# A 32-byte tile ahead of all others on the right-hand side of SBUF

## The chip, the cores and the metric

The kernel runs on one core of a Trainium2 chip. The metric is the time of one execution on the device, in microseconds. Before the change the median of three runs is 992.73 us (992.7 to 994.15).

## The reference

Three layers follow each other, all in float32.

```
phi(x) = exp(h - max h) / sqrt(128),  h = x @ omega.T - |x|^2/2      # 4 x 8 heads, 576 tokens, 64 wide
num, den = phi(q) @ (phi(k).T @ v),  phi(q) @ sum phi(k)
x = num / (den + 1e-6)                                               # 2304 tokens x 512
h = x @ w_in;  x = (max(h,0) + alpha * min(h,0)) @ w_out             # hidden width 2048
out = ((x @ w_a) * (x @ w_b)) @ w_out                                # hidden width 1536
```

## The kernel before

Every large product keeps float32 accuracy by splitting each operand into a high and a low part (`hi`, `lo`, type float32r) and adding three products, high x high, high x low and low x high. A hidden tile of 128 columns costs 12 matmuls in the first layer (line 440: four 128-row pieces of x, three products each) and 12 in the second (line 498). Such twelve are called a block below. The weights of both MLPs come in as raw bits and are taken apart by a decoder (the class at line 165) on GpSimd, VectorE and ScalarE into slots, each `[128, 2, 512]` float32r: high part first, low part 2048 bytes behind it.

The work goes through four stages.

- 0 to about 256 us: linear attention (lines 651 to 758) with the first MLP's earliest chunks between its steps, 256 tokens at a time (object `A`, pools on the left).
- Up to about 551 us: the rest of the first MLP (object `X`, line 994), in chunks of 512 tokens and one of 256. Two chunks of 512 use hidden tiles 0 to 7; then four of 512 and one of 256 use hidden tiles 8 to 15.
- Up to 988 us: the second MLP, in 3 x 3 rounds. In each, two calls of `dual` make 7 products of 12 matmuls with 384 columns (line 1067); `back` then makes six groups of 12 matmuls with 512 columns (line 1138), which read a weight slot as the moving operand and the 384-column tiles `gh` and `gl` as the stationary one.

The order of every engine is the program's own order (`manual_schedule`); queues and waits follow from it.

Where the tiles lie is decided by pools. SBUF is filled from two sides. On the left stand the constants, the weight slots 0 to 16 (pool `w1`), the decoder's tiles, x, and the pools of object `A`; in the second MLP also the x pieces of the products A11, S1 and S2 (pool `xa`). On the right, from the top downwards, stand all attention tiles; after them the weight slots 17 to 24 (`w2`) and all pools of object `X`; after these the slots 25 and 26 (`w3`) and the other pools of the second MLP. Each stage's pools are stacked from the same top.

Which slot a weight tile q has is said by `place`: q below 20 has slot q, 20 to 24 have 20 to 24, and 25 to 31 have slots 0 to 6. Hidden tile f of the first MLP uses q = 2f in line 440 and q = 2f + 1 in line 498. So hidden tiles 0 to 7 lie wholly in left slots; of tiles 8 to 15, q = 17 to 24 lie on the right and the other eight on the left. In the second MLP the four slots that `back` reads are 4, 5, 6 and 25 in the first three rounds, 3 to 6 in the next three, 2 to 5 in the last three.

Of the kernel before, what the change touches and what calls it, by code (L numbers as in the profile page):

```python
# [9 lines left out]
F32 = mybir.dt.float32  # L10
# [8 lines left out]
P = 128  # L19
# [40 lines left out]
def tile_kernel(ctx: ExitStack, tc: tile.TileContext, qT, kT, v1, omT, wbits, alpha, out):  # L60
    nc = tc.nc
    ctx.enter_context(tc.manual_schedule())
    scale = 1.0 / math.sqrt(math.sqrt(D))

    const = ctx.enter_context(tc.tile_pool(name="const", bufs=1))
    w1 = ctx.enter_context(tc.tile_pool(name="w1", bufs=1))
    dec = ctx.enter_context(tc.tile_pool(name="dec", bufs=2))
# [1116 lines left out]
RIGHT = "right"  # L1184
# [54 lines left out]
```

## Time and profile before

| what | us |
|---|---|
| median of three runs | 992.73 |
| the profiled execution | 989.9 |
| its span, first to last instruction | 988.1 |
| TensorE busy (matmuls) | 954.2, 97% |
| VectorE, ScalarE, GpSimd busy | 698.9, 445.0, 381.9 |

The profile has one execution. The chain of work that ended last tells at each moment which instruction the end of the program hung on. A block of matmuls there shows the rate at which TensorE works through its stream: its time divided by the number of matmuls. (The duration of one matmul in the lists of groups is longer than that, since matmuls overlap.)

### The profile page before, as it was taken

The page shows a single profiled execution, that of the slowest core. Times are in us where ns is not written, and L with a number is a line of the kernel's source. Part 1 is how long each engine was busy: PE and PEld are TensorE (multiplying, and loading weights), DVE is VectorE, ACT ScalarE, POOL GpSimd, SP SyncE. Part 2 cuts the span into 40 slices and gives each one's busy share as a digit, 9 for nine tenths or more (in the row PEclk, how much of TensorE's full clock was granted, in tenths as well). Part 3 has the DMA queues.
Part 4 walks back from the last instruction along what each step waited for, and adds up shares of the span by engine and source line. Part 5 has one row for each costly group of instructions (what it writes and reads, how often), then busy time and mean ns, then how long its engine had stood idle before and what let it go on. Part 6 is the DMA issues. An engine that isn't in the chain of part 4 may idle for free.

```text
span 988.1 us, 16903 instructions
## 1 busy us (share of the span) xinstructions
PE 954.2 (97%) x6486; PEld 848.7 (86%) x6486; DVE 698.9 (71%) x1276; ACT 445.0 (45%) x1094; POOL 381.9 (39%) x312
## 2 busy tenths in 40 slices
PE   8899999999999999998999989999999999999998
PEld 7788889999888888888888879899989898979796
DVE  5888855554547768688667988799588995573733
ACT  5877766654444443333333344443343431333340
POOL 3676700000066655437325646264155272030300
PEclk8999999999999999999999999999999999999999
DMA  8544323000123242424546657159827378613112
GB/s 292 175 148 162 113 74 98 24 1 23 43 78 99 80 150 64 135 79 143 198 136 245 233 216 259 62 191 381 292 106 266 118 265 324 242 54 139 63 66 96
DMA packets 54177, 146.55 MB, mean 148 GB/s; under 512 B 5072, under 2 KB 11472, under 8 KB 54096
## 3 DMA queue, kind: packets, MB, share of 16 engines
q1 hardware_dynamic: 53952, 145.34, 42.3%
q8 instruction: 51, 0.84, 0.3%
q14 instruction: 30, 0.25, 0.1%
q10 hardware_dynamic: 144, 0.13, 0.0%
HBM read 98.79 MB, written 46.66 MB: 147 GB/s over the span
## 4 chain that ended last, share of the span: by engine, by line
PE 78%; DVE 13%; ACT 5%; issue 2%; DMA 2%; POOL 0%; SPq 0%; ACTq 0%; DVEq 0%; POOLq 0%
PE y L498 19%; PE h L440 18%; PE o L1138 12%; PE W L1067 12%; PE E L1067 7%; ACT ph L684 3%; PE B L1067 2%; DVE sumS L163 2%; DVE s L163 2%; PE tp L712 1%; DVE e L163 1%; PE kv L697 1%; PE nd L731 1%; DVE gl L163 1%; DMA out<-opl 1%
## 5 line engine op out<-in xcount | busy, mean ns | idle before, releaser
L498 PE MATMUL y<-gh,w 128*128 128x256 f32 (+1 forms) x768 | 205.0, 342 | 3.7 <-ACT gh L468 3.6
L440 PE MATMUL h<-xh,w 128*128 128x256 f32 (+1 forms) x768 | 206.1, 342 | 1.0 <-ACT xh L425 1.0
L196 POOL TENSOR_SCALAR z<-raw 128x512 f32<-128x512 f32 x68 | 111.3, 1639 | 136.7 <-DMA raw<-in_w 75.4
L498 PEld LDWEIGHTS y<-gh,w 128*128 128x128 f32 x768 | 135.4, 191 | 21.1 <-ACT gh L468 4.5
L440 PEld LDWEIGHTS h<-xh,w 128*128 128x128 f32 x768 | 135.1, 189 | 18.1 <-ACT xh L425 1.2
L1138 PE MATMUL o<-w,gh 128*128 128x512 f32 x432 | 137.0, 399 | 0.0
L498 PE MATMUL y<-gl,w 128*128 128x512 f32 (+1 forms) x384 | 130.7, 340 | 0.9 <-DVE gl L465 0.8
L231 POOL TENSOR_TENSOR a<-a,w 128x512 f32<-128x512 f32 x32 | 48.4, 1512 | 213.5 <-ACT w L230 210.7
L440 PE MATMUL h<-xl,w 128*128 128x512 f32 (+1 forms) x384 | 130.1, 339 | 0.5 <-DVE xl L429 0.5
L457 DVE SCALAR_TENSOR_TENSOR h<-u,nalpha,h 128x256 f32<-128x256 f32 (+1 forms) x96 | 59.5, 620 | 83.3 <-ACT h L456 82.2
L1138 PEld LDWEIGHTS o<-w,gh 128*128 128x128 f32 x432 | 81.4, 190 | 19.5 <-ACT gh L155 1.5
L1138 PE MATMUL o<-w,gl 128*128 128x512 f32 x216 | 86.6, 401 | 11.3 <-DVE gl L163 11.3
L455 ACT ACTIVATE u<-h 128x256 f32<-128x256 f32 (+1 forms) x96 | 47.1, 491 | 103.1 <-PE h L440 102.9
L468 ACT ACTIVATE gh<-h 128x256 fp32r<-128x256 f32 (+1 forms) x96 | 47.1, 491 | 99.4 <-DVE h L457 99.4
L498 PEld LDWEIGHTS y<-gl,w 128*128 128x128 f32 x384 | 73.2, 191 | 9.9 <-DVE gl L465 1.6
L440 PEld LDWEIGHTS h<-xl,w 128*128 128x128 f32 x384 | 72.8, 190 | 9.4 <-DVE xl L429 1.0
L465 DVE TENSOR_TENSOR gl<-h,gh 128x256 fp32r<-128x256 f32 (+1 forms) x96 | 53.2, 554 | 24.6 <-ACT gh L468 24.4
L155 ACT ACTIVATE u<-W 128x384 f32<-128x384 f32 x72 | 35.0, 492 | 68.4 <-PE W L1067 67.7
L1138 PEld LDWEIGHTS o<-w,gl 128*128 128x128 f32 x216 | 41.0, 190 | 23.5 <-DVE gl L163 13.9
L217 DVE SCALAR_TENSOR_TENSOR a<-raw,z 128x512 uint32<-128x512 uint32 x68 | 55.6, 818 | 1.9
L221 DVE SCALAR_TENSOR_TENSOR c<-raw,c 128x512 f32<-128x512 uint32 x68 | 49.6, 730 | 2.3
L163 DVE TENSOR_TENSOR opl<-o,opl 128x512 f32<-128x512 f32 x36 | 24.7, 686 | 34.1 <-DMA opl<-opart 25.2
(512 smaller groups left out, 2071.8 us busy)
## 6 DMA issues: line engine op xcount, KB each, us to landing
raw<-in_w SPq DMA_DIRECT2D x68, 512.0 KB, 4.6
w<-store SPq DMA_DIRECT2D x44, 512.0 KB, 7.0
store<-t_None SPq DMA_DIRECT2D x39, 512.0 KB, 2.9
st<-ypart SPq DMA_DIRECT2D x14, 768.0 KB, 6.9
opl<-opart SPq DMA_DIRECT2D x36, 256.0 KB, 3.0
v<-in_v SPq DMA_DIRECT2D x8, 650.0 KB, 5.8
q<-in_qT SPq DMA_DIRECT2D x8, 576.0 KB, 3.7
opart<-op SPq DMA_DIRECT2D x18, 256.0 KB, 2.8
```

Of the source, the lines that this page charges most:

```text
L163: nc.vector.tensor_tensor(out=out, in0=in0, in1=in1, op=op)
L196: nc.gpsimd.tensor_scalar(out=z.bitcast(F32), in0=self.raw[i][:, :, 1].bitcast(F32), scalar1=2.0 ** -112, scalar2=None, op0=ALU.mult)
L217: stt(out=a, in0=H, scalar=0x80000000, in1=z, op0=ALU.bitwise_and, op1=ALU.bitwise_or)
L221: stt(out=c, in0=L, scalar=2.0 ** -52, in1=c, op0=ALU.mult, op1=ALU.mult)
L231: eng.tensor_tensor(out=a, in0=a, in1=hi.bitcast(F32), op=ALU.subtract)
L440: nc.tensor.matmul(hp, lhsT=w_[:, ks], rhs=r_, start=(i == 0), stop=(i == 3 * KT - 1))
L455: nc.scalar.activation(u_, hp, AF.Relu, scale=-1.0)
L457: nc.vector.scalar_tensor_tensor(out=hp, in0=u_, scalar=nalpha[:, f:f + 1], in1=hp, op0=ALU.mult, op1=ALU.add)
L465: nc.vector.tensor_tensor(out=gl, in0=hp, in1=gh.bitcast(F32), op=ALU.subtract)
L498: nc.tensor.matmul(ys[e], lhsT=w_[:, es], rhs=r_, start=(first and i == 0 and head), stop=(last and i == 2 and tail))
L1067: nc.tensor.matmul(out, lhsT=w_[:, ks], rhs=r_, skip_group_check=True, start=(i == 0 and nm in ("A11", "S1", "A12")), stop=(i == 5))
L1138: nc.tensor.matmul(ob, lhsT=w_[:, cs], rhs=r_, start=(n == 0), stop=(n == 11))
```

## The change

A pool `pad` is opened first on the right-hand side, with one tile of eight float32 (32 bytes) in each partition. Nothing reads or writes it.

```diff
     scale = 1.0 / math.sqrt(math.sqrt(D))
 
+    ctx.enter_context(tc.tile_pool(name="pad", bufs=1, side=RIGHT)).tile([P, 8], F32, name="pad")
     const = ctx.enter_context(tc.tile_pool(name="const", bufs=1))
     w1 = ctx.enter_context(tc.tile_pool(name="w1", bufs=1))
```

The order of instructions on each engine, and what each waits for, is the same in both built programs. What differs is the address of each tile on the right: 32 bytes less. The built programs have these start addresses in a partition (remainders of the division by 64 and by 512; all tiles of a kind that is listed have the same remainder, and the steps inside them, 512, 1024, 1536 and 2048 bytes, keep them):

```
tiles                                              by 64          by 512
                                                before  after  before  after
left:  slots 0-16, x, pools of A, pool xa            0      0     192    192
right: slots 17-26, pools of X, all other
       tiles of the second MLP                      32      0     480    448
right, attention: ph, phT, xn, k, first v            0     32     192    160
right, attention: q, ident                           0     32     384    352
left:  om (the scaled omega, a view into x)          0      0     448    448
```

So before the change an operand on the left and one on the right stood 32 bytes apart (by 64) in the two MLPs; now they agree. In the attention the projections (line 661) read `om` on the left as the moving operand and `k` or `q` on the right as the stationary one: these agreed, and now stand 32 bytes apart. The other attention matmuls have both operands on the right.

## Rows read from the trace of the kernel before

**Rows 1.** The page: span, and the chain that ended last, by engine and line.
```profile
span 988.1 us, 16903 instructions
...
PE 78%; DVE 13%; ACT 5%; issue 2%; DMA 2%; POOL 0%; SPq 0%; ACTq 0%; DVEq 0%; POOLq 0%
PE y L498 19%; PE h L440 18%; PE o L1138 12%; PE W L1067 12%; PE E L1067 7%; ACT ph L684 3%; PE B L1067 2%; DVE sumS L163 2%; DVE s L163 2%; PE tp L712 1%; DVE e L163 1%; PE kv L697 1%; PE nd L731 1%; DVE gl L163 1%; DMA out<-opl 1%
```
**Rows 2.** Groups by shape: count, busy us, mean ns, idle before.
```profile
L440 PE MATMUL h<-xh,w 128*128 128x512 f32 x384 | 126.9, 394 | 1.0 <-ACT xh L425 1.0
L498 PE MATMUL y<-gh,w 128*128 128x512 f32 x384 | 126.9, 394 | 0.1
```
**Rows 3.** Chain that ended last, first MLP, 512 tokens: start us, us, what.
```profile
347.85 2.80 PE y L498 x12
350.65 5.44 PE h L440 x24
356.09 2.72 PE y L498 x12
...
369.70 2.79 PE h L440 x12
```
**Rows 4.** The same chain, first MLP, the chunk of 256 tokens.
```profile
433.38 1.40 PE h L440 x12
...
437.58 2.87 PE h L440 x24
440.45 1.44 PE y L498 x12
```
**Rows 5.** The same chain, second MLP: 384 columns (E, W), 512 columns (o).
```profile
577.67 2.13 PE W L1067 x12
...
607.72 2.08 PE E L1067 x12
...
638.95 14.42 PE o L1138 x61
...
682.53 16.71 PE o L1138 x72
```
**Rows 6.** The same chain in the last six rounds, three of five pieces of `back`.
```profile
733.11 14.50 PE o L1138 x61
...
825.10 16.79 PE o L1138 x72
...
923.32 14.50 PE o L1138 x61
```
**Rows 7.** The same chain at the program's end.
```profile
970.85 3.34 DMA out<-opl
...
978.24 3.18 DMA out<-opl
...
981.43 2.81 DMA opl<-opart
```
**Rows 8.** Windows, line 468 alone (ScalarE, 256 columns): window, length, busy us, count.
```profile
60.00:256.00 196.00, 14.19 (x37) 1.00 0.21 69
433.00:465.00 32.00, 3.07 (x8) 0.95 0.37 124
```
**Rows 9.** Windows, line 465 alone (VectorE, 256 columns).
```profile
60.00:256.00 196.00, 15.91 (x38) 1.00 0.21 69
433.00:465.00 32.00, 3.36 (x8) 0.95 0.37 124
```
**Rows 10.** Windows, line 661 alone (projections): PE busy, PEld busy.
```profile
0.00:60.00 60.00, 20.26 (x220) 16.51 (x220) 0.94 0.67 231
60.00:256.00 196.00, 29.04 (x356) 23.20 (x356) 1.00 0.21 69
```
**Rows 11.** Waits of TensorE, longest in total first: us, times, longest.
```profile
PE o L1138 <- DVE gl L163: 11.3, 6, 3.3
PE y L498 <- ACT gh L468: 3.6, 2, 3.3
```

## The prediction

> **What bounds the kernel now.** I read the page's chain first: 78% of the span lies on TensorE, and the first MLP's two lines, 498 and 440, hold 37% of it, line 1138 another 12% [rows 1]. Then I followed the chain in order of time and divided each piece by its matmuls, since a change of addresses can only move time by changing how long something takes. The reader is to see that the same work has two rates. In the first MLP with 512 columns, a block of 12 takes 2.80 us in some places and 2.72 us (5.44 for two) in others, within 30 us, with full clock and no idle time between [rows 3]. With 256 columns it takes 1.40 us, or 1.44 us (2.87 for two) [rows 4]. With 384 columns nearly all blocks read 2.08, a few 2.13 [rows 5].
>
> What goes with the two rates is found by naming the weight slot of each block in rows 3. The chunk begins with hidden tile 8, whose first-layer weight is q = 16, a left slot; the pieces at 347.85 (the chunk before, left slots) and 369.70 (q = 26, slot 1) read left slots as well: 2.80 and 2.79. The pieces at 350.65 (tiles 9 and 10, q = 18 and 20) and 356.09 (tile 8's second layer, q = 17) read right slots: 2.72 a block. The moving operand is on the right throughout. So left weights under a right moving operand, 32 bytes apart by 64, go at 2.80, and right under right, no distance, at 2.72. In the chunk of 256 the piece at 433.38 (q = 16, left) takes 1.40, the two from 437.58 (q = 18 and 20) and the one at 440.45 (q = 17), all right, 1.44. I take this as one rule: with no distance a block of 512 columns is 0.08 us quicker, one of 256 is 0.04 us dearer, one of 384 is the same. Rows 5 fit: a full `back` of 72 matmuls in the first three rounds, one slot in four on the right, takes 16.71, which is 2.785 for 12 (a quarter at 2.72 and the rest at 2.80 would make 2.78); in the later rounds, with all four slots on the left under stationary tiles on the right, 16.79, or 2.798 [rows 6]. So the distance costs the same whichever operand is on the left.
>
> **The change part by part.** It adds no instruction and no wait, and moves none. It takes the distance between left and right in the MLPs from 32 to 0 by 64 bytes. Each term is a count of blocks times one of these differences.
>
> First MLP, 512 columns: the two chunks on tiles 0 to 7 have 16 blocks each in left slots, the four on tiles 8 to 15 have 8 each (q = 16 and 25 to 31), 32 + 32 = 64 of the 96 blocks that the counts give (384 matmuls high x high and high x low plus half as many with the low moving part, for each of two lines [rows 2]). 64 x 0.08 = 5.1 us less. All on the path: TensorE waits 3.6 us for line 498 in this stage and hardly otherwise [rows 11], and the decoder's work is due in the same order of instructions, so it moves forward with TensorE.
>
> First MLP, 256 columns: 8 blocks in left slots, 8 x 0.04 = 0.3 us more. The earlier 256-column chunks have both operands on the left and keep their addresses.
>
> Second MLP, line 1138: at the matched rate 72 matmuls take 6 x 2.72 = 16.32. A full group in the first three rounds loses 16.71 - 16.32 = 0.39, in the later ones 0.47. Where the chain has 61 of 72, because the first eleven run while VectorE still makes `gl`, 61/72 of that counts: 0.33 and 0.40. The chain has 61 twice in the first three rounds (one of them in rows 5), 72 once: 0.33 x 2 + 0.39 = 1.05. Of the last six rounds five are on the chain, four with 61 and one with 72 [rows 6]: 4 x 0.40 + 0.47 = 2.07. In the last round nothing is won: its chain is a row of transfers, out and back in (3.34, 3.18, 2.81), not matmuls [rows 7]. Sum 3.1 us less.
>
> Second MLP, 384 columns: 126 blocks (9 rounds x 14), on either side 2.08 [rows 5]: nothing. The few at 2.13 may go or come.
>
> Attention projections: they lose their match, and no row shows this shape at both distances. It is 220 + 356 = 576 matmul records [rows 10]. The nearest rows are blocks of 256 columns (0.04 us less per 12 when apart) and of 512 (0.08 more): -1.9 to +3.8 us if all were on the path. A third shape, 384, shows no effect and lies between them; I take 0 and keep both ends.
>
> Everything else that touches right-hand tiles: ScalarE's line 468 takes 14.19/37 = 0.384 us on the left and 3.07/8 = 0.384 on the right [rows 8], VectorE's line 465 15.91/38 = 0.419 and 0.420 [rows 9]: the 32 bytes do nothing there, so 0. GpSimd and the transfers I cost at nothing; TensorE's stream covers both, except at the end, where three transfers out and one back in follow each other. The two out-transfers of rows 7 differ by 0.16 us though their tiles have the same remainder, so the end may move by 4 x 0.16 = 0.6 us either way.
>
> Sum: -5.1 + 0.3 - 3.1 = -7.9 us, on the profiled execution's 989.9 (span 988.1): 982.0. That execution was 2.8 us below the median of the timed runs, 992.73; the same 7.9 off the median gives 984.8, which I forecast. Its own range, with a projection cost of up to +2 and rounding of 0.08 by 0.005 over the 64 + 40 blocks (0.5 us): 983 to 987.
>
> The Trainium skill speaks against this. "SBUF — State Buffer", section "Who interferes with whom", gives TensorE two independent read ports, one for the moving operand and one for weight loads, and says that it never waits on anyone; by that the distance between the two operands cannot matter, and the sum is 0 instead of -7.9. The two rates in rows 3 disagree with that reading, on one engine with the same instructions.
>
> **The rivals.**
>
> The gain is met by new waits. In the second MLP each `back` starts after VectorE has made `gl`: TensorE already waits 11.3 us for that [rows 11], and VectorE has the decoder's work between. If VectorE's stream set the rounds, the 3.1 us would turn into longer waits; left are -5.1 + 0.3 = -4.8, so 987.9. Against it: the chain runs through `back` in eight rounds of nine, and the VectorE work ahead of it starts when TensorE ends the product before.
>
> Nothing happens. The rates may hang on a distance by more than 64 bytes: left and right stood 288 bytes apart by 512, and will stand 256 apart. If only a multiple of 512 matches, all blocks stay: 992.7. The trace has no pair 256 bytes apart in this data type, so it can't exclude that. For the forecast: steps of 512 to 2048 bytes inside the slots change nothing, and 32 bytes is what is odd about 288. The skill's ports end here too.
>
> Slower, by one mechanism: 256 bytes is a worse distance than 288. Then the 512-column blocks stay at 2.80, and the 384-column ones, which today read 2.08 at 288, drop to the 2.13 that some show: 75 blocks with a left and a right operand (4 of 7 products take x from the right, of whose 72 blocks 3 have weights in slot 25 or 26; 6 blocks have it the other way round) x 0.05 = 3.8 us: 996.5. It decides if blocks of 384 columns after 600 us read 2.12 or more.
>
> More: the projections gain as 256-column blocks do (-1.9) and the blocks at 2.13 go to 2.08: about 982.5.
>
> **How the numbers follow.** Chances: forecast 0.57, new waits 0.14, nothing 0.14, slower 0.09, more 0.06. A measurement of this kernel can tell 0.2%, 2.0 us, from no change. Forecast, new waits and more are faster: 0.77; nothing is the same: 0.14; slower 0.09. The range of 8 in 10 reaches from 981.5, which takes in the case of more, over forecast and new waits to 993.5, most of the case of nothing; the slower case is left out.
>
> **What would show it.** In the chain of the changed kernel, the 64 left-slot blocks of 512 columns at 2.72 instead of 2.80, from about 258 us on; the left-slot blocks of 256 at 1.44; full `back` groups at 16.3; blocks of 384 still at 2.08; ScalarE and VectorE groups unchanged in mean. The stage from 256 to 553 us should be 4.8 us shorter, the attention before it as long as now. The forecast is wrong if the blocks stay at 2.80 (then the distance counts by 512), if the first 256 us grow by more than 2 us, or if the wait of line 1138 for `gl` grows from 11.3 us by what the blocks gain.

## The result and the profile after

The changed kernel takes 983.84 us in the median of six runs (981.82 to 985.89), the kernel before 992.99 us beside it (991.39 to 994.47). The ratio is 0.9907 with a 95% interval of 0.9888 to 0.9925: 9.2 us faster, somewhere between 7.4 and 11.1. The forecast was 7.9 us less, 984.8 us. The profiled executions, 989.9 and 982.27 us, differ by 7.6.

The page of the changed kernel answers to [rows 1]. Every line number of the program is one higher than before.

```profile
span 980.5 us, 16903 instructions
...
PE 78%; DVE 11%; ACT 5%; DMA 3%; issue 2%; POOL 0%; SPq 0%; ACTq 0%; DVEq 0%; POOLq 0%
```

The number of instructions is the same and the shares are close to those before (VectorE 13 and now 11%, transfers 2 and 3%). What has changed is the rate. The chain that ended last in the first MLP, 512 columns (start us, us, what), with the blocks that answer to [rows 3]:

```profile
345.04 2.72 PE y L499 x12
347.76 5.44 PE h L441 x24
353.20 2.72 PE y L499 x12
...
366.80 2.72 PE h L441 x12
```

The first and the last read left slots and were at 2.80 and 2.79; the two between read right slots and stay at 2.72. Left and right can't be told apart any more. The same chain in the chunk of 256 tokens, as [rows 4]:

```profile
429.36 1.43 PE h L441 x12
...
433.54 2.87 PE h L441 x24
```

Here the left-slot block is dearer, 1.43 after 1.40, as the sum had it. The second MLP, as [rows 5] and [rows 6]:

```profile
573.13 2.09 PE W L1068 x12
...
635.19 14.12 PE o L1139 x61
...
678.46 16.36 PE o L1139 x72
...
728.56 14.10 PE o L1139 x61
...
819.24 16.36 PE o L1139 x72
```

Full groups of `back` took 16.71 and 16.79 and now both take 16.36; those of 61 took 14.42 to 14.50 and now 14.10 to 14.12. The block of 384 columns that was at 2.13 in [rows 5] is at 2.09. The end answers to [rows 7]:

```profile
963.32 3.29 DMA out<-opl
...
973.63 2.96 DMA opl<-opart
```

It starts 7.5 us earlier (970.85 before) and has the same transfers (the two that are not shown here take 3.13 and 3.10).

Where the time was won is read at the borders of the stages. Three pieces of the chain before, which stand at the start of the 512-column chunks, at the first MLP's last block and at the first `back`:

```profile
258.22 8.43 PE h L440 x35
...
551.02 2.82 PE y L498 x11
...
589.87 15.74 PE o L1138 x61
```

and the same three after:

```profile
257.94 8.22 PE h L441 x35
...
546.54 2.79 PE y L499 x11
...
586.10 15.77 PE o L1139 x61
```

The attention stage ends 0.28 us earlier. The first MLP's 512-column part wins another 4.48 - 0.28 = 4.2. From there to the first `back` 4.48 - 3.77 = 0.7 is given back, and from the first `back` to the end's first transfer 7.53 - 3.77 = 3.8 is won.

The groups that were to be indifferent are so. A window of line 469 alone, ScalarE with 256 columns, as [rows 8]: window, length, busy us and count, then granted clock, busy share of the transfer engines and GB/s. From 430 to 462 us it takes 3.08 for 8. VectorE's line 466, as [rows 9], takes 15.79 for 38 and 3.35 for 8.

```profile
60.00:256.00 196.00, 14.19 (x37) 1.00 0.21 69
```

And of line 662 alone, the projections (PE, then PEld), as [rows 10].

```profile
60.00:256.00 196.00, 29.01 (x356) 23.18 (x356) 1.00 0.21 69
```

29.04 before and 29.01 after, where the clock was full both times. The first 60 us differ with the granted clock: 20.26 at 0.94 before, 19.86 at 0.97 after.

### The profile page after: what moved, and what is told of

It is laid out like the page before. It is cut to its first block, busy times and chain, and to the rows that moved or that the text cites. A ratio compares the mean times of both kernels' runs of the same rounds, so it can differ in the third digit from the quotient of the medians.

```text
span 980.5 us, 16903 instructions
## 1 busy us (share of the span) xinstructions
PE 944.2 (96%) x6486; PEld 846.6 (86%) x6486; DVE 697.0 (71%) x1276; ACT 444.4 (45%) x1094; POOL 381.5 (39%) x312
## 4 chain that ended last, share of the span: by engine, by line
PE 78%; DVE 11%; ACT 5%; DMA 3%; issue 2%; POOL 0%; SPq 0%; ACTq 0%; DVEq 0%; POOLq 0%
PE y L499 19%; PE h L441 18%; PE W L1068 13%; PE o L1139 12%; PE E L1068 7%; ACT ph L685 2%; PE B L1068 2%; DVE sumS L164 2%; DVE s L164 1%; DMA v<-in_v 1%; PE tp L713 1%; PE nd L732 1%; PE kv L698 1%; DMA out<-opl 1%; DVE e L164 1%
## 5 line engine op out<-in xcount | busy, mean ns | idle before, releaser
L499 PE MATMUL y<-gh,w 128*128 128x256 f32 (+1 forms) x768 | 202.5, 338 | 4.0 <-ACT gh L469 4.0
L1139 PE MATMUL o<-w,gh 128*128 128x512 f32 x432 | 134.9, 394 | 0.0
```

Of the source, the lines that this page charges most:

```text
L499: nc.tensor.matmul(ys[e], lhsT=w_[:, es], rhs=r_, start=(first and i == 0 and head), stop=(last and i == 2 and tail))
L1139: nc.tensor.matmul(ob, lhsT=w_[:, cs], rhs=r_, start=(n == 0), stop=(n == 11))
```

## The experiments

**32 bytes on the left instead.**

```diff
+    ctx.enter_context(tc.tile_pool(name="lpad", bufs=1)).tile([P, 8], F32, name="lpad")
     const = ctx.enter_context(tc.tile_pool(name="const", bufs=1))
```

> The 32 bytes go to the head of the left-hand side; the right-hand tiles keep their old addresses. Distance theory (the moving and the stationary operand of a matmul must have the same remainder by 64): left and right agree again, both 32 past a multiple of 64, so left-slot blocks of 512 columns take 2.72 us and the ratio to the kernel before is 0.990 to 0.993. Rival, own place (a right-hand tile must itself start at a multiple of 64): nothing on the right has moved and the left has lost its place, so blocks of 512 stay at 2.80 or more and the ratio is 1.000 or above. Rival, attention (the gain comes from moved attention tiles): ratio 1.000.

Measured: 0.9913 (0.9887 to 0.9939). The chain at a left-slot block and the two right-slot blocks behind it:

```profile
345.61 2.72 PE y L499 x12
348.33 5.44 PE h L441 x24
```

No right-hand tile has moved, and the gain can't be told from the changed kernel's. A place of its own that the right-hand side had to have is out. A share of the attention is not out by this run: `om` lies on the left, so the distance in the projections changed here too.

**32 bytes on both sides.**

```diff
+    ctx.enter_context(tc.tile_pool(name="pad", bufs=1, side=RIGHT)).tile([P, 8], F32, name="pad")
+    ctx.enter_context(tc.tile_pool(name="lpad", bufs=1)).tile([P, 8], F32, name="lpad")
     const = ctx.enter_context(tc.tile_pool(name="const", bufs=1))
```

> 32 bytes on either side: the right-hand tiles stand as in the changed kernel, at a multiple of 64, the left-hand ones 32 past it. Distance theory: the distance is back, left-slot blocks of 512 columns take 2.80 us, ratio 0.999 to 1.001. Rival, own place: the right-hand tiles stand well, so the gain stays, 2.72 us and 0.991.

Measured: 1.0002 (0.9984 to 1.0019).

```profile
348.53 2.80 PE y L500 x12
351.33 5.46 PE h L442 x24
```

Left-slot blocks are back at 2.80, right-slot ones stay at 2.72 or 2.73. The two edits that each win 0.9% alone win nothing together: it is the distance (32 again, now with the left 32 past the right).

**64 bytes on the right.** The change with a tile of `[P, 16]` in place of `[P, 8]`.

> 64 bytes instead of 32 on the right: the remainder by 64 is what it was before, by 512 it is 416 against 192 on the left. Distance theory by 64: 2.80 us again, ratio 1.000. Rival, any shift of the right-hand tiles away from their old place gains (by 256 or 512, or by an accident of the old place): 2.72 us or another rate, ratio 0.991 or something else than 1.000.

Measured: 0.9999 (0.9982 to 1.0017); left-slot blocks at 2.80. The distance is wrong again and the gain is gone, so it isn't that any move away from the old place helps.

**288 bytes on the right.** The same with `[P, 72]`.

> 288 bytes on the right: all operands of the two MLPs have the same remainder by 512, 192. Distance theory by 64: as the changed kernel, 2.72 us and a ratio of 0.990 to 0.992. Rival, distance by 256 or 512 (the changed kernel, 256 apart, has only part of what can be had): blocks of 512 below 2.72 us and a ratio under 0.989.

Measured: 0.9919 (0.9899 to 0.9938), blocks at 2.72. A distance of 0 by 512 gives no more than the changed kernel's 256. The rival of the prediction by which only a multiple of 512 matches had fallen with the result itself; this shows that nothing was left to win there.

**The attention tiles alone.**

```diff
+    rpool(st_a, name="pad", bufs=1).tile([P, 8], F32, name="pad")
     ac = rpool(st_a, name="ac", bufs=1)
```

> The 32 bytes stand only under the attention tiles and are given back with them; both MLPs have their old addresses. Forecast theory: the projections are indifferent, ratio 0.999 to 1.001, blocks of 512 columns at 2.80 us. Rival, the attention has a share in the gain (the measured 9.1 us are more than the forecast 7.9, and the profiled attention stage was 0.3 us shorter): ratio 0.998 or below.

Measured: 0.9985 (0.9968 to 1.0002). The left-slot blocks stay at 2.80, and no gain can be told; a share of up to 0.3% can't be excluded by this run alone.

**Both MLPs alone.**

```diff
+    xpool(RIGHT, name="pad", bufs=1).tile([P, 8], F32, name="pad")
     st_w = ExitStack()
```

> The 32 bytes are put on the right only after the attention tiles have been given back: both MLPs as in the changed kernel, the attention as before. Forecast theory: the whole gain, ratio 0.990 to 0.992. Rival, attention has a share: 0.993 or above.

Measured: 0.9907 (0.9881 to 0.9934), the changed kernel's own ratio. The gain lies in the MLPs.

**TensorE alone, 24 pairs of distances.** The loop of the experiment, with `d` and `s` the bytes of the moving and of the stationary operand past a multiple of 512 from the tile's start:

```
    for n, tag in ((512, "c"), (256, "a"), (384, "b")):
        for d, s, name in CASES:
            ...
            for b in range(3):
                ...
                for k in range(4):
                    xh, xl = part(0, d, n), part(1024, d, n)
                    wh, wl = part(2048 + 128 * k, s, P), part(3072 + 128 * k, s, P)
                    for w_, r_ in ((wh, xh), (wh, xl), (wl, xh)):
                        nc.tensor.matmul(o, lhsT=w_, rhs=r_, start=(i == 0), stop=(i == 11))
```

> TensorE alone: 36 matmuls for each of 24 pairs of distances and of 512, 256 and 384 columns, with float32r operands in one tile; nothing of the reference is computed and the output is zeros. Distance theory: 226.7 ns a matmul with 512 columns and 120.0 with 256 wherever moving and stationary operand have the same remainder by 64 (0, 64, 128, 192, 256, and 32 under 32, 16 under 16), about 233 and 117 at 32, 96, 160, 224, 288 and 480; 384 columns 173.3 throughout. What the other distances (4 to 60 bytes) do the theory doesn't say; if the rate hung on a shared 32-byte or 16-byte line instead, 16 would stand with 0 or with 32. Rival, a rule by 256 or 512: 64, 128 and 192 differ from 0.

Measured in one execution, in the chain: 36 matmuls each. The names end in c for 512 columns and a for 256; the letter before is the case: a is 0 over 0, d 16, f 32, j 60, k 64, m 128, o 192, q 256 over 0, u 32 over 32, v 16 over 16.

```profile
17.44 8.16 PE vac L47 x36
...
59.24 8.39 PE vfc L47 x36
...
92.72 8.18 PE vjc L47 x36
100.90 8.24 PE vkc L47 x36
...
117.55 8.40 PE vmc L47 x36
...
134.38 8.40 PE voc L47 x36
...
151.17 8.19 PE vqc L47 x36
...
184.54 8.16 PE vuc L47 x36
192.71 8.32 PE vvc L47 x36
...
222.12 4.32 PE vaa L47 x36
...
235.07 4.08 PE vda L47 x36
...
243.47 4.20 PE vfa L47 x36
...
281.82 4.10 PE voa L47 x36
```

Divided by 36: 226.7 ns at 0 and at 32 over 32, 227.5 at 256 (with a few slower ones at its start), 233.1 at 32, which are the 2.72 and 2.80 of the kernel without any other engine at work. So far as expected. But 128 and 192 agree with 0 by 64 and take 233.3, and 64 takes 228.9: the rule by 64 is wrong. Of the distances that are multiples of 32, as all in the kernel are, only 0 and 256 go at the quick rate, and 64 comes near: among these the rule is one by 256. It is no rule for all addresses: 60 over 0 takes 227.2, as quick as 256, and 16 over 16 takes 231.1 where 0 over 0 takes 226.7. With 256 columns it takes 120.0 at 0 and least, 113.3, at 16.

**96 bytes on the right**, which separates the two rules in the kernel itself: `[P, 24]`.

> 96 bytes on the right: left and right agree by 64 (both 0), but stand 192 apart by 256. The forecast's rule, remainder by 64: left-slot blocks of 512 columns at 2.72 us, ratio 0.991. The rule by 256, which the run with TensorE alone suggests (226.7 ns at distances 0 and 256, 233.3 at 128 and 192): 2.80, ratio 1.000.

Measured: 0.9992 (0.9975 to 1.0009). A left-slot block, the two on the right, and a left one again:

```profile
348.28 2.80 PE y L499 x12
351.08 5.47 PE h L441 x24
...
370.15 2.80 PE h L441 x12
...
827.99 16.48 PE o L1139 x72
```

All tiles of the two MLPs start at multiples of 64 bytes, the left-slot blocks stay at 2.80, and no gain in the time can be told. By 64 is refuted in the kernel too. The last line is one thing that the expectation didn't name: in `back` the moving operand stands 64 past the stationary one by 256, and a full group of the later rounds takes 16.48 instead of 16.79, which is 72 times the 228.9 ns of TensorE alone at 64. In the first three rounds it takes 16.70 instead of 16.71; why it gains nothing there is open.

**224 bytes on the right**: `[P, 56]`.

> 224 bytes on the right: left and right agree by 64 and stand 64 apart by 256. Rule by 64: 2.72 us and 0.991. Rule by 256 as the run with TensorE alone has it (228.9 ns at 64): blocks with the moving operand 64 past the stationary one at 2.75, ratio 0.993 to 0.997; the matmuls of the second MLP's last product have it the other way round (192) and stay at 2.80.

Measured: 0.9964 (0.9948 to 0.9980).

```profile
346.51 2.75 PE y L499 x12
...
824.45 16.79 PE o L1139 x72
```

The 64 left-slot blocks at 2.75 instead of 2.80 are worth 64 x 0.05 = 3.2 us, or 0.9968; `back`, where the moving operand is 192 past the stationary one by 256, keeps its 16.79. A distance of 64 gives part of the gain, by the size that TensorE alone had shown.

**The early chunks 32 bytes off their weights**, on top of the change.

```diff
+    st_m.enter_context(tc.tile_pool(name="apad", bufs=1, reuse_waits="pool")).tile([P, 8], F32, name="apad")
     A = Mlp(st_m, CI, 2)
```

> The changed kernel with another 32 bytes on the left ahead of the pools that hold the operands of the first MLP's earliest 256-column chunks (80 blocks, run between the attention's steps): these now stand 32 bytes from their weights. Distance theory: such a block takes 1.40 instead of 1.44 us; where the stage hangs on TensorE throughout, 80 x 0.04 = 3.2 us less, ratio to the kernel before 0.987; where ScalarE's and VectorE's attention work sets the stage, nothing, 0.991. I expect something between, 0.988 to 0.990. Rival, 256 columns are as quick at either distance and the 1.40 of the one chunk was its neighbours' doing: 1.44, 0.991.

Measured: 0.9896 (0.9872 to 0.9920), not to be told from the changed kernel. Two blocks, and the start of the 512-column chunks:

```profile
226.23 2.81 PE y L499 x24
...
257.00 8.23 PE h L441 x35
```

The block's rate did come (2.81 for two; 2.87 for such a pair where the distance is 0), but 80 x 0.035 = 2.8 us of it show as 0.9 us at the stage's end, 257.94 in the changed kernel. Summed piece by piece, the chain up to there has 97 us of such blocks, 64 us of the attention's matmuls and 42 us each of VectorE and ScalarE, so the stage does not hang on these blocks throughout; where the other 1.9 us went is not shown.

**All 256-column blocks 192 bytes off their weights**, the attempt to beat both: the edit before with `[P, 48]`, and in `X` each tile of a 256-token chunk taken 48 elements further.

```diff
+        def off(self, n):
+            return 0 if self.pair or n == self.cap else 48
...
-            hi = self.px.tile([P, self.cap], F32R, tag="xh", name=f"xh{ph}_{o}_{k}")[:, :n]
+            hi = self.px.tile([P, self.cap], F32R, tag="xh", name=f"xh{ph}_{o}_{k}")[:, self.off(n):self.off(n) + n]
```

> An attempt to beat both kernels: the changed kernel, with the operands of all 256-column blocks of the first MLP 192 bytes past their weights by 256, where TensorE alone took 113.3 ns a matmul instead of 120.0. Distance rule by 256: 1.36 us a block instead of 1.44, 96 blocks, so up to 7.7 us less if these stages hung on TensorE throughout, ratio 0.983. The run with a distance of 32 in the early chunks had 117.0 ns and began the 512-column stage only 0.3 us earlier, so I expect nearly nothing: 0.988 to 0.991.

Measured: 0.9893 (0.9875 to 0.9911); its interval covers the changed kernel's 0.9907, so it is not shown to be better. (The expectation misread two numbers: 113.3 ns was the rate at 16, at 192 it was 113.9; and the 512-column stage had begun 0.9 us earlier than in the changed kernel, not 0.3.) In the chunk of 256:

```profile
428.41 1.41 PE h L444 x12
```

1.41 us is 117.5 ns a matmul and not the 113.9 that TensorE alone had at this distance. With 256 columns the distance alone doesn't say the rate.

## Why the prediction was right, and where it was not

The bound was read rightly. The MLPs hang mostly on TensorE, and the addresses of the operands set its rate; the 64 blocks of 512 columns came from 2.80 to 2.72, worth 5.1 us, or 4.8 with the dearer blocks of 256. The border shows 4.2. "All on the path" did not hold at the end of this stage, where the chain runs over VectorE, ScalarE and a transfer of raw weights, before and after:

```profile
541.69 3.85 DMA raw<-in_w
...
537.04 4.09 DMA raw<-in_w
```

TensorE is busy 0.33 us less there (11.68 and 11.35), yet the stretch takes 12.54 us (534.00 to 546.54) after 12.37 (538.65 to 551.02). Another 0.2 is lost in the blocks behind TensorE's wait in the chunk of 256.

Line 1138 was to give 3.1. The full groups gave 0.35 and 0.43 (forecast 0.39 and 0.47), those of 61 in the later rounds 0.37 to 0.40 (0.40), the second piece of the first three rounds 0.30 (0.33). The very first gave nothing, 15.74 and 15.77. Its windows, TensorE alone, before and after (the first number behind the count is the granted clock):

```profile
589.87:605.62 15.75, 15.75 (x62) 0.91 0.40 152
...
586.10:601.87 15.77, 15.77 (x62) 0.89 0.46 168
```

The clock was low at its start in both: 0.54 over the first 3.1 us before and 0.62 over the first 4.5 us after, mostly the lower level, 1.2 GHz. TensorE had waited 3.3 us ahead of it before and 4.2 us after. Once the clock is full, three matmuls take 0.70 us before and 0.68 after, so the rate came here too, and the longer stretch at the low clock took it back. In the run with 32 bytes on the left the clock is full throughout this piece (1.00), and the same 61 take 14.16:

```profile
586.13 14.16 PE o L1139 x61
```

No term of the sum stood for the clock.

The stretch ahead of this piece took back 0.7 us more (38.85 and 39.56): VectorE was busy for most of it, 35.0 and 35.7 us, and TensorE waited for it longer. That is the rival of the new waits, in one place of eight. Its sign is seen in the wait of line 1139 for `gl`:

```profile
PE o L1139 <- DVE gl L164: 12.2, 6, 4.2
```

11.3 before [rows 11].

The term for 384 columns was mis-sized. I took 0, since nearly all blocks read 2.08. From the first `back` on 3.8 us were won; the seven `back` pieces after the first give 0.30 + 0.35 + 0.40 + 0.37 + 0.43 + 0.38 + 0.38 = 2.6 (some of these pieces are not shown here). The other 1.2 lies between and behind them. 0.4 of it is in the one stretch ahead of a `back`, from 748 us, where the chain before ran over VectorE for longer; the remaining 0.8 is in stretches that hold 384-column blocks which were not at 2.08, such as this pair, before and after:

```profile
711.79 4.22 PE W L1067 x24
...
707.32 4.16 PE W L1068 x24
```

The case "more" had named them and given them hardly a number. Why they were dearer is open: TensorE alone takes 173.3 to 173.6 ns with 384 columns at 0, 32, 224 and 288, 2.08 a block.

So that the sum came out at 7.9 and the profiled executions 7.6 apart is in part luck. The first MLP gave 0.6 less than forecast, line 1138 0.5 less, and 0.7 was given back ahead of it; against that stand the 1.2 and the 0.28 of the attention stage, which the change is not shown to have caused.

The attention's projections cost nothing, as taken: the run with the attention tiles alone and the window of line 662 show no cost.

The step that failed, though the time came out, is the rule itself. I said that the distance counts by 64 bytes, because "32 bytes is what is odd about 288" and steps of 512 to 2048 change nothing. Those rows only showed that multiples of 512 don't count; any rule by 64, 128, 256 or 512 fits them, and the change moves the distance to 256, at which the first three agree. That the change lands on 256, the distance that goes as quickly as 0, was luck. The runs with 96 and 224 bytes show it; either would have been forecast at 0.991 by my rule, and they gave 0.9992 and 0.9964.

The sum of 0, drawn from the Trainium skill, "SBUF — State Buffer", section "Who interferes with whom", did not come. The section speaks of what engines do to each other and calls TensorE's two read ports independent; that the distance of its own two operands can't matter was my inference. The run with TensorE alone speaks against that: the same instructions, no other engine at work from 17.4 us on, 226.7 or 233.1 ns by the distance of the two operands. That ports are what is met there is not shown by any run.

## What to carry to other kernels

Where one line of matmuls shows two steady rates in the chain, name the addresses of both operands by remainder before looking for a wait; here a distance of 0 or 256 bytes gave the quick one, and 32 bytes moved a tuned kernel by 0.9%. Pools that are stacked from two ends don't share their remainders, and a tile of 32 bytes is enough to change that. A rule read from a trace that holds only two distances should be tried on a third, away from the kernel, before it is used for a design.

## What the runs showed of the hardware

At the full granted clock, 2.4 GHz in the run with TensorE alone, a matmul with float32r operands and a weight load of its own takes as long as its columns and 32 more at one column a cycle with both operands at 0 (0 over 0): 226.7, 173.3 and 120.0 ns for 512, 384 and 256. At 256 over 0 they take 227.5, 174.2 and 119.7. Apart by 32 the 512 columns take 233.1 ns, 6.4 more, and the 256 columns 116.7 ns, 3.3 less: what is a loss with long moving operands is a gain with short ones. With 384 columns the rate is 173.3 at 0 and at 32:

```profile
330.50 6.24 PE vab L47 x36
...
361.90 6.24 PE vfb L47 x36
...
399.48 6.36 PE vlb L47 x36
```

(a is 0, f is 32, l is 96 over 0, 176.7 ns.) Why 32 and 96 differ there, why 60 over 0 goes as quickly as 256 over 0 and 16 over 16 more slowly than 0 over 0 with 512 columns, and why 256 columns at 192 took 113.9 ns alone and 117.5 in the kernel, stays open.
